# Four moves of order in a fused attention and mixture-of-depths kernel: a query transfer, a scatter, a ranking and a selection

## The chip, the cores and the metric

The kernel runs on one core of a Trainium2 chip. The metric is the device time of one execution in microseconds (us). Each kernel is run several times and the median is given. One further execution is recorded by the hardware profiler; all places in time below count from the first instruction of that record.

The engines are TensorE (PE, with its weight loads as PEld), VectorE (DVE), ScalarE (ACT), GpSimd (POOL) and SyncE (SP). Each works through its own queue in the order in which the program was written, and they wait for one another by semaphores. Transfers are issued from a queue of SP, ACT or POOL and run on 16 DMA engines.

## The reference, cut to what matters

All is float32. Eight batches, eight heads, 1152 keys of 64 values; 576 pooled queries. Then 128 of the 576 rows of each batch are chosen by a score, and go through two layers.

```python
q_pool = q.reshape(B, H, S // 2, 2, D).mean(axis=3)
scores = np.matmul(q_pool, k.transpose(0, 1, 3, 2)) / np.sqrt(D)
attn = np.exp(scores - np.max(scores, axis=-1, keepdims=True))
attn = attn / (np.sum(attn, axis=-1, keepdims=True) + 1e-09)
x = np.matmul(attn, v)                      # (B,H,S,D) -> (B, S, H*D)
scores = np.einsum('bsd,d->bs', x, w_gate)
out = x.copy()
for b in range(B):
    top_idx = np.argpartition(-scores[b], capacity)[:capacity]
    xe = x[b, top_idx]
    ye = np.maximum(xe @ w1, 0.0) @ w2
    g = 1.0 / (1.0 + np.exp(-scores[b, top_idx]))
    out[b, top_idx] = x[b, top_idx] + g[:, None] * ye
```

## The kernel before, in words

The class `_Plain` does the work; `_any_scores` is a second version behind a branch and does not run with these inputs.

**Halves.** The main loop in `run` goes over 32 pairs of heads (four to a batch), each cut into two halves of 288 pooled queries: 64 halves, numbered h. In half h TensorE computes the scores (L877, 72 matmul records), ScalarE takes their exponentials out of PSUM (L884), and TensorE forms the weighted values of half h - 1 (L895, 72 records), which ScalarE copies out (L903, tile `two`) and GpSimd adds up (L905, tile `av`). For the sums of the exponentials, GpSimd adds units of p in three instructions (L916, tile `acc`), DVE folds p and acc (L921) and reduces (L931, tile `sum`); ScalarE lays these side by side (L946, tile `groups`), DVE adds (L952), ScalarE spreads (L961). Further DVE and GpSimd steps transpose (L974), multiply by the gate weights (L984), reduce (L1042) and divide (L1020, tile `x`), and SP stores x to DRAM (L1031). In the first half of each pair the next pair is prepared: GpSimd adds the two rows of each query (L775, `qp`), DVE transposes keys and queries (L778 `kT`, L782 `qT`). There are four PSUM tiles of two banks.

**Order of the work beside it.** What belongs to the choice of rows is written as generators (`routed`, then `layers_of_two`). Three places in each half move them on: "mid" (after the scores), "sums" (after the folds) and "end". `units` takes a generator to its next truthy yield; what it yields says at which place it goes on, and `True` stands for "end". So one more `yield True` moves all that follows by half a pair. In `ending`, after the loop, `pieces(unit, n)` moves a generator by n yields by hand.

**Choosing the rows.** For each batch `routed` sends the 576 scores through DRAM so that they come back shifted per partition (L1089, L1092, tile `line`). The rank of a row is the number of larger scores, counted by ten DVE comparisons, two for each of five tiles t of rows (L1121). For batches 0 to 6 rank and gate go through DRAM (L1150 `row_rank`, L1154 `lines`), and DVE searches in `lines` which row has a given rank (L1185, twice, once with the constant table `token_line`, which holds the number of each row). GpSimd gathers the rows (L1212, `xe`), SP sends them to DRAM and reads them back (L1225 `copy`, L1242), DVE transposes (L1250). For the last batch, 7, DVE builds a matrix of comparisons `pick` in one instruction (L1162), and TensorE multiplies it with `meta`, the number and the gate of each row (L1171, pick stationary, two columns moving); ScalarE copies index and gate (L1178, L1179).

**Layers and scatter.** Batches 0 and 1, and 2 and 3, go through both layers in pairs (`layers_of_two`, seven products in place of eight, L1346). At its end each of the two tokens is scaled and added (`scaled`, L1435), and GpSimd scatters it into out (`written`, L1288); then the sums of weights for the next first layer are loaded again (`load_sums`, L721). Batches 4 to 7 are done in `ending` (L1421 first layer, L1431 second layer), where the products of the second layer come from the generator `second`, and y1, y2, y7 are the places of products 1, 2 and 7.

**Start.** `load_first` loads the first pair without the general path: queries in two parts of three transfers each (L803), keys as three and six columns of both heads (L811), values (L815). `first_queries` (L823, L830, L836, L837) and `first_keys` (L844, L851) add and transpose them.

**Batch 6's place.** With `cuts` of 2 for batch 6, the comparisons of tiles 0 to 2 are written at the end of one half, the others at "mid" of the next, so that all ten stand together in DVE's queue, before the folds of that half.

Of the kernel before, what the change touches and what calls it, by code (L numbers as in the profile page):

```python
# [13 lines left out]
G = 3  # L14
# [525 lines left out]
class _Plain:  # L540
# [85 lines left out]
    def constants(self):  # L626
        nc, const = self.nc, self.const

        token_i = self.small.tile([P, self.NT], I32, name="token_i")
        nc.gpsimd.iota(token_i[:, :], pattern=[[P, self.NT]], base=0, channel_multiplier=1)  # L630
        self.token = const.tile([P, self.NT], F32, name="token")
        nc.vector.tensor_copy(self.token[:, :], token_i[:, :])

        line_i = self.ffn.tile([P, P, 2, self.NT], I32, name="lines", bufs=1)[:, :, 0, :]
        nc.gpsimd.iota(line_i, pattern=[[1, P], [P, self.NT]], base=0, channel_multiplier=0)
        self.token_line = const.tile([P, P, self.NT], F32, name="token_line")
        nc.gpsimd.tensor_copy(self.token_line[:, :, :], line_i)
# [146 lines left out]
    def load_first(self, b, hp):  # L784


        nc, NC, D = self.nc, self.NC, self.D
        room = self.work.tile([P, self.NG, G, 2, self.HALF], F32, name="p")
        room = room.rearrange("p g u j n -> p (g u j n)")
        sixth, n_k = self.QB // 6, 2 * NC * D  # L790
        kn = room[:, 0:n_k].rearrange("p (c j d) -> p c j d", c=NC, j=2)
        n_q = 2 * 4 * sixth * D
        qn = room[0 : 3 * BLK, n_k : n_k + n_q].rearrange("p (a j m d) -> p a j m d", a=2, j=2, d=D)
        qp = room[0 : 3 * BLK, n_k + n_q : n_k + n_q + n_q // 2]
        qp = qp.rearrange("p (a n j d) -> p a n j d", a=2, j=2, d=D)
# [4 lines left out]
        def queries(engine, half):  # L800

            for g in range(3):
                engine.dma_start(  # L803
                    qn[g * BLK : (g + 1) * BLK, half].rearrange("i j m d -> i j (m d)"), of[3 * half + g]
                )

        queries(nc.scalar, 0)
        for a, z in ((0, G), (G, NC)):
            for j, h in enumerate(heads):
                keys = self.k[b, h].rearrange("(p c) d -> p c d", c=NC)  # L810
                nc.sync.dma_start(kn[:, a:z, j, :], keys[:, a:z, :])  # L811
        queries(nc.sync, 1)
        for j, h in enumerate(heads):
            of = self.v[b, h].rearrange("(p c) d -> p c d", c=NC)
            nc.sync.dma_start(v_sb[:, j, :, :], of)  # L815
        return {"k": kn, "q": qn, "qp": qp, "v": v_sb, "b": b, "hp": hp}
# [248 lines left out]
    def routed(self, b, part):  # L1065
# [33 lines left out]
        if b < self.B - 2:  # L1099
            yield True  # L1100
        gate = ffn.tile([P, NT], F32, name="gate")

        small = nc.vector if b == self.B - 1 else nc.gpsimd
        small.tensor_scalar(
            out=gate[:, :], in0=sc, scalar1=-88.0, scalar2=None, op0=ALU.max
        )

        if b == self.B - 1:
            nc.scalar.activation(gate[:, :], gate[:, :], AF.Exp, scale=-1.0)
            yield True  # L1110
        parts = ffn.tile([P, NT, 2], F32, name="rank_parts")
        nc.vector.memset(parts[:, :, :], 0.0)

        nc.vector.memset(parts[self.TAIL :, NF, :], float(Sp))
        rank = ffn.tile([P, NT], F32, name="rank")
        cuts = {self.B - 2: (2,), self.B - 1: (NT,)}.get(b, (1, 3))
        for t, rows in tiles:
            own = t * P + P - 1
            cmp = ffn.tile([P, NT, P], F32, name="pick", bufs=1).rearrange("p t n -> p (t n)")
# [17 lines left out]
        small.tensor_scalar(  # L1137
            out=gate[:, :], in0=gate[:, :], scalar1=1.0, scalar2=None, op0=ALU.add
        )
        if b == self.B - 1:  # L1140
# [15 lines left out]
        for s0, w in self.slots:  # L1156
            index = ffn.tile([P, 1], I32, name="index", bufs=4)
            own_gate = ffn.tile([P, 1], F32, name="own_gate", bufs=4)
            if b == self.B - 1:

                pick = ffn.tile([P, NT, P], F32, name="pick", bufs=1)
                nc.vector.tensor_tensor(  # L1162
                    out=pick[:, :, 0:w],
                    in0=self.token_line[:, s0 : s0 + w, 0].unsqueeze(1).broadcast_to([P, NT, w]),
                    in1=rank[:, :].unsqueeze(2).broadcast_to([P, NT, w]),
                    op=ALU.is_equal,
                )
                yield True
                ps = self.banks()[:, 0, 0:2]
                for t, rows in tiles:  # L1170
                    nc.tensor.matmul(  # L1171
                        ps[0:w, :],
                        lhsT=pick[0:rows, t, 0:w],
                        rhs=meta[0:rows, t, :],
                        start=(t == 0),
                        stop=(t == NT - 1),
                    )
                nc.scalar.copy(index[0:w, :], ps[0:w, 0:1])  # L1178
                nc.scalar.copy(own_gate[0:w, :], ps[0:w, 1:2])  # L1179
            else:  # L1180
# [12 lines left out]
                    )  # L1193

                found = self.small.tile([P, 1], F32, name="found_token")
                search(self.token_line, found)
                nc.vector.tensor_scalar(
                    out=index[0:w, :],
                    in0=found[0:w, :],
# [161 lines left out]
    def layers_of_two(self, tokens):  # L1361
# [148 lines left out]
    def ending(self, halves, old):  # L1510
# [29 lines left out]
        self.gated(halves[-1])  # L1540
        self.scored(halves[-1])
        _, new, _ = self.routing.pop()
        pieces(new, 1)
        pieces(layer, 2)
        for of in (halves[-3]["pair"], last):
# [271 lines left out]
```

## Time and profile before

| | us |
|---|---|
| median of 3 runs | 684.45 |
| lowest, highest | 683.55, 685.75 |
| the profiled execution | 683.79 |
| its span, first to last instruction | 682.0 |
| TensorE busy | 671.3 |
| VectorE busy | 566.1 |
| GpSimd busy | 499.6 |
| ScalarE busy | 454.0 |

The span is what the record covers; 1.8 us of the profiled execution's time lie around it. A line of the timeline gives the start, the time, the engine, the line of the kernel, the operation, the tile written and the tiles read, and how many instructions are merged in it; in brackets the engine's idle time before it and what ended that. A float32 matmul leaves two records. Records of L877 and L895 overlap, since four of them run in different quarters of the array: 72 of them take about 4.37 us though each lasts 0.4.

### The profile page before, as it was taken

How to read it: one execution, taken by the hardware profiler on the slowest of the kernel's cores; microseconds unless marked ns; L12 is line 12 of the kernel's file. 1: busy time of each engine (PE TensorE's matmuls, PEld its weight loads, DVE VectorE, ACT ScalarE, POOL GpSimd, SP SyncE). 2: the span in 40 equal slices, each digit the busy share in tenths (PEclk: the TensorE clock that was granted, in tenths of full speed). 3: DMA queues.
4: the chain of work that ended last, by engine and by line, in shares of the span. 5: the costliest groups of instructions: out<-in, count | busy, mean ns of one | idle time of the engine just before them, and what ended most of it. 6: DMA issues, size and time to landing. Idle time of an engine off the chain costs nothing.

```text
span 682.0 us, 23423 instructions
## 1 busy us (share of the span) xinstructions
PE 671.3 (98%) x9953; PEld 456.7 (67%) x9953; DVE 566.1 (83%) x814; ACT 454.0 (67%) x989; POOL 499.6 (73%) x474
## 2 busy tenths in 40 slices
PE   8999999999999999999999999999999999999996
PEld 6666666665666568676667767767666775657995
DVE  3878998998999887686899987686889998788874
ACT  5677777777877773856777778483777777774220
POOL 4778888889888883866798888384879888867011
PEclk9999999999999999999999999999999999999999
DMA  8888888859896884753888788374588978562311
GB/s 164 168 185 186 221 177 194 160 99 194 197 190 114 175 159 89 202 97 83 225 189 167 146 165 165 81 179 83 122 244 167 161 146 178 129 175 67 64 39 36
DMA packets 391785, 101.99 MB, mean 150 GB/s; under 512 B 371576, under 2 KB 375544, under 8 KB 390648
## 3 DMA queue, kind: packets, MB, share of 16 engines
q1 hardware_dynamic: 390152, 95.93, 66.9%
q0 software_dynamic: 1280, 4.20, 1.8%
q8 instruction: 79, 1.29, 0.8%
q10 hardware_dynamic: 240, 0.30, 0.2%
q14 instruction: 34, 0.28, 0.1%
HBM read 82.77 MB, written 17.62 MB: 147 GB/s over the span
## 4 chain that ended last, share of the span: by engine, by line
PE 79%; DVE 6%; POOL 5%; issue 4%; DMA 3%; ACT 1%; ACTq 0%; POOLq 0%; DVEq 0%
PE ps L877 35%; PE ps L895 35%; PE ps L1346 7%; POOL acc L916 3%; DVE pick L1121 2%; DMA xe<-out_dram,index 1%; PE ps L1421 1%; ACT p L884 1%; DVE kT L778 1%; PE ps L1431 1%; POOL qp L775 1%; DMA p<-in_q_dram 1%; DVE fold L921 1%; POOL out_dram L1288 1%; POOL prod L984 0%
## 5 line engine op out<-in xcount | busy, mean ns | idle before, releaser
L884 ACT ACTIVATE p<-ps 128x576 f32<-128x576 f32 x576 | 320.4, 696 | 4.0 <-PE ps L877 4.0
L916 POOL TENSOR_TENSOR acc<-p 128x576 f32<-128x576 f32 x192 | 275.8, 1465 | 35.1 <-ACT p L884 34.7
L877 PE MATMUL ps<-qT,kT 64*64 64x288 f32 x4608 | 294.0, 404 | 2.1 <-DVE qT L782 1.1
L895 PE MATMUL ps<-p,v_sb 64*64 64x288 f32 x4608 | 291.6, 403 | 0.0
L877 PEld LDWEIGHTS ps<-qT,kT 64*64 64x64 f32 x4608 | 178.1, 132 | 105.7 <-ACT p L884 18.8
L895 PEld LDWEIGHTS ps<-p,v_sb 64*64 64x64 f32 x4608 | 178.2, 133 | 101.3 <-ACT p L884 13.5
L921 DVE TRANSPOSE_TENSOR_REDUCE fold<-p 128x54 f32<-128x1728 f32 x64 | 126.1, 1971 | 39.8 <-ACT p L884 39.8
L921 DVE TRANSPOSE_TENSOR_REDUCE fold<-acc 128x54 f32<-128x1728 f32 x64 | 124.7, 1948 | 17.2 <-POOL acc L916 16.8
L903 ACT COPY two<-ps 128x576 f32<-128x576 f32 x64 | 40.8, 638 | 132.1 <-PE ps L895 127.4
L905 POOL TENSOR_TENSOR av<-two 128x288 f32<-128x288 f32 x64 | 51.2, 800 | 70.7 <-ACT two L903 70.5
L778 DVE STREAM_TRANSPOSE kT<-kb 128x1152 f32<-128x1152 f32 x31 | 73.2, 2360 | 0.0
L984 POOL TENSOR_TENSOR prod<-avb,w_gate 128x288 f32<-128x288 f32 x64 | 51.1, 799 | 0.7 <-DVE red L1042 0.5
L1121 DVE TENSOR_SCALAR_CACHE_REDUCE pick<-line 128x127 f32<-128x127 f32 (+4 forms) x80 | 45.3, 566 | 2.4
L775 POOL TENSOR_TENSOR qp<-qb 128x576 f32<-128x576 f32 x31 | 43.7, 1411 | 2.8 <-DMA qb<-in_q_dram 2.8
L974 DVE STREAM_TRANSPOSE avb<-av 128x288 f32<-128x288 f32 x64 | 28.4, 444 | 18.5 <-POOL av L905 18.5
L961 ACT ACTIVATE sums<-total,tiny 32x18 f32<-32x18 f32 x124 | 38.2, 308 | 5.5 <-DVE total L952 3.6
L1020 POOL TENSOR_TENSOR x<-avb,rec 128x576 f32<-128x576 f32 x30 | 34.8, 1160 | 0.0
L946 ACT COPY groups<-sum 32x36 f32<-32x36 f32 x124 | 27.2, 219 | 5.1 <-DVE sum L931 3.3
L1042 DVE TENSOR_REDUCE red<-prod 128x9 f32<-128x288 f32 x64 | 27.8, 435 | 0.1
L931 DVE TENSOR_REDUCE sum<-fold 128x18 f32<-128x108 f32 x64 | 21.9, 342 | 2.2
L1288 POOL DMA_INDIRECT out_dram<-xe,index x7 | 8.4, 1198 | 20.8 <-DVE xe L1435 10.3
L782 DVE STREAM_TRANSPOSE qT<-qp 128x576 f32<-128x576 f32 x31 | 23.0, 741 | 0.0
(166 smaller groups left out, 437.9 us busy)
## 6 DMA issues: line engine op xcount, KB each, us to landing
kb<-in_k_dram SPq DMA_DIRECT2D x124, 144.0 KB, 3.9
qb<-in_q_dram SPq DMA_DIRECT2D x124, 144.0 KB, 3.6
v_sb<-in_v_dram SPq DMA_DIRECT2D x31, 576.0 KB, 4.8
out_dram<-x SPq DMA_DIRECT2D x128, 72.0 KB, 4.6
tw<-tw SPq DMA_DIRECT2D x8, 1024.0 KB, 6.1
lines<-row_rank SPq DMA_DIRECT2D x7, 640.0 KB, 4.1
w<-in_moe_w_dram SPq DMA_DIRECT2D x8, 512.0 KB, 5.1
tw<-tw SPq DMA_DIRECT2D x8, 512.0 KB, 5.8
```

The lines of the kernel that those rows point to most:

```text
L775: nc.gpsimd.tensor_tensor(out=qp[:, :, :], in0=pair["q"][:, :, 0, :], in1=pair["q"][:, :, 1, :], op=ALU.add)
L778: nc.vector.transpose(kT.rearrange("p (c i g) -> p c g i", c=self.NC, i=BLK), pair["k"].rearrange("p (g c) d -> p c g d", c=self.NC),)
L877: nc.tensor.matmul(sc[keys, j, 0:n], lhsT=pair["kT"][rows, c * P + keys.start : c * P + keys.stop], rhs=pair["qT"][rows, qs], start=True, ...
L884: nc.scalar.activation(p[:, c // G, c % G, :, :], sc[:, :, 0:n], AF.Exp, scale=self.scale)
L895: nc.tensor.matmul(av[j * self.D : (j + 1) * self.D, e, 0:n], lhsT=half["pair"]["v"][keys, j, c, :], rhs=half["p"][keys, c // G, c % G, j, :],
L903: nc.scalar.copy(two[:, :, :], av[:, :, 0:n])
L905: nc.gpsimd.tensor_tensor(out=half["av"][:, :], in0=two[:, 0, :], in1=two[:, 1, :], op=ALU.add)
L916: nc.gpsimd.tensor_tensor(out=acc[:, u, :], in0=units[:, 0, u, :], in1=units[:, 1, u, :], op=ALU.add)
L921: nc.vector.tensor_reduce(fold[:, a, :], of.rearrange("p u (m d) -> p (u m) d", d=BLK), AX.X, ALU.add, apply_transpose=True,)
L984: self.nc.gpsimd.tensor_tensor(out=pair["prod"][:, ns, :], in0=pair["avb"][:, ns, :], in1=self.w_gate[:, hp : hp + 1, :].broadcast_to([P, ...
L1121: nc.vector.tensor_scalar(out=cmp[0:rows, 0 : part.stop - part.start], in0=near[0:rows, part], scalar1=sc[0:rows, t : t + 1], scalar2=None ...
L1346: nc.tensor.matmul(args[0], lhsT=args[1], rhs=args[2], start=k == 0, stop=k == n - 1)
```

## The change

- The third transfer of the first half's queries is issued from SP, between the two small and the two large key transfers, and not from ScalarE's queue.
- `token_line` lies as [tile, place] and not as [place, tile]; the search reads it through a rearranged view.
- The second token of a pair is scattered one half later, by one more `yield True`; the loads behind it go with it.
- Batch 6's comparisons are cut after tile 1, and the rest goes to the end of the next half, not to its "mid". All later steps of batch 6 come a half later, so that the gather is the last step in the loop, and `ending` takes one more piece of it.
- Batch 7: two small gate operations go from DVE to GpSimd, two memsets come earlier; `pick` is made by five comparisons, and stands as the moving operand with `meta` as the stationary one; the result of two rows is copied to SBUF and transposed back. In `ending` product 7 of the second layer comes after these matmuls and before the transpose.

```diff
-        self.token_line = const.tile([P, P, self.NT], F32, name="token_line")
-        nc.gpsimd.tensor_copy(self.token_line[:, :, :], line_i)
+        self.token_line = const.tile([P, self.NT, P], F32, name="token_line")
+        nc.gpsimd.tensor_copy(self.token_line.rearrange("p t i -> p i t"), line_i)
...
-        queries(nc.scalar, 0)
-        for a, z in ((0, G), (G, NC)):
...
-        queries(nc.sync, 1)
+        queries(nc.scalar, 0, (0, 1))
+        keys(0, G)
+        queries(nc.sync, 0, (2,))
+        keys(G, NC)
+        queries(nc.sync, 1, range(3))
...
-        small = nc.vector if b == self.B - 1 else nc.gpsimd
-        small.tensor_scalar(
+        nc.gpsimd.tensor_scalar(
             out=gate[:, :], in0=sc, scalar1=-88.0, scalar2=None, op0=ALU.max
         )
...
-        cuts = {self.B - 2: (2,), self.B - 1: (NT,)}.get(b, (1, 3))
+        cuts = {self.B - 2: (1,), self.B - 1: (NT,)}.get(b, (1, 3))
...
             if t == cuts[-1]:
-                yield "mid"
+                yield mid
...
-                nc.vector.tensor_tensor(
-                    out=pick[:, :, 0:w],
-                    in0=self.token_line[:, s0 : s0 + w, 0].unsqueeze(1).broadcast_to([P, NT, w]),
-                    in1=rank[:, :].unsqueeze(2).broadcast_to([P, NT, w]),
-                    op=ALU.is_equal,
-                )
+                for t, rows in tiles:
+                    nc.vector.tensor_scalar(
+                        out=pick[0:rows, t, 0:w],
+                        in0=self.token_line[0:rows, 0, s0 : s0 + w],
+                        scalar1=rank[0:rows, t : t + 1],
+                        scalar2=None,
+                        op0=ALU.is_equal,
+                    )
                 yield True
-                ps = self.banks()[:, 0, 0:2]
+                ps = self.banks()[:, 0, :]
                 for t, rows in tiles:
                     nc.tensor.matmul(
-                        ps[0:w, :],
-                        lhsT=pick[0:rows, t, 0:w],
-                        rhs=meta[0:rows, t, :],
+                        ps[0:2, 0:w],
+                        lhsT=meta[0:rows, t, :],
+                        rhs=pick[0:rows, t, 0:w],
                         start=(t == 0),
                         stop=(t == NT - 1),
                     )
+                found = ffn.tile([P, NT, P], F32, name="pick", bufs=1)[0:2, 0, 0:w]
+                nc.scalar.copy(found, ps[0:2, 0:w])
+                yield True
+                ps = self.banks()[:, 0, 0:2]
+                nc.tensor.transpose(ps[0:w, :], found, self.ident[0:2, 0:2])
...
             yield True
+            if token is tokens[1]:
+                yield True
             self.written(token, token["index"])
...
         pieces(old, 1)
         pieces(new, 1)
...
-        for to in (y1, y2, y7):
+        for to in (y1, y2):
             copy(to, next(second))
...
         pieces(new, 2)
+        copy(y7, next(second))
+        pieces(new, 1)
         pieces(layer)
```

In the last but one place, the line `pieces(old, 1)` ahead of `pieces(new, 1)` is the one that is added.

More of the change, by code (lines that the diff above doesn't have):

```diff
@@ L798, in load_first, with queries @@
         of = self.q[b, 2 * hp : 2 * hp + 2].rearrange("j (i t m) d -> t i j (m d)", i=BLK, t=6)
-        def queries(engine, half):
-            for g in range(3):
+        def queries(engine, half, groups):
+            for g in groups:
                 engine.dma_start(
@@ L805, in queries, with keys @@
                 )
-        queries(nc.scalar, 0)
-        for a, z in ((0, G), (G, NC)):
+        def keys(a, z):
             for j, h in enumerate(heads):
-                keys = self.k[b, h].rearrange("(p c) d -> p c d", c=NC)
-                nc.sync.dma_start(kn[:, a:z, j, :], keys[:, a:z, :])
-        queries(nc.sync, 1)
+                rows = self.k[b, h].rearrange("(p c) d -> p c d", c=NC)
+                nc.sync.dma_start(kn[:, a:z, j, :], rows[:, a:z, :])
+        queries(nc.scalar, 0, (0, 1))
[3 more added lines that the diff above has]
+        queries(nc.sync, 1, range(3))
         for j, h in enumerate(heads):
@@ L1101, in routed @@
         gate = ffn.tile([P, NT], F32, name="gate")
-        small = nc.vector if b == self.B - 1 else nc.gpsimd
-        small.tensor_scalar(
+        nc.gpsimd.tensor_scalar(
             out=gate[:, :], in0=sc, scalar1=-88.0, scalar2=None, op0=ALU.max
         )
+        parts = ffn.tile([P, NT, 2], F32, name="rank_parts")
+        nc.vector.memset(parts[:, :, :], 0.0)
+        nc.vector.memset(parts[self.TAIL :, NF, :], float(Sp))
         if b == self.B - 1:
@@ L1110, in routed @@
             yield True
-        parts = ffn.tile([P, NT, 2], F32, name="rank_parts")
-        nc.vector.memset(parts[:, :, :], 0.0)
-        nc.vector.memset(parts[self.TAIL :, NF, :], float(Sp))
         rank = ffn.tile([P, NT], F32, name="rank")
-        cuts = {self.B - 2: (2,), self.B - 1: (NT,)}.get(b, (1, 3))
+        cuts = {self.B - 2: (1,), self.B - 1: (NT,)}.get(b, (1, 3))
         for t, rows in tiles:
@@ L1136, in routed @@
                     yield True
-        small.tensor_scalar(
+        nc.gpsimd.tensor_scalar(
             out=gate[:, :], in0=gate[:, :], scalar1=1.0, scalar2=None, op0=ALU.add
@@ L1195, in routed @@
                 found = self.small.tile([P, 1], F32, name="found_token")
-                search(self.token_line, found)
+                search(self.token_line.rearrange("p t i -> p i t"), found)
                 nc.vector.tensor_scalar(
@@ L1542, in ending @@
         _, new, _ = self.routing.pop()
+        pieces(old, 1)
         pieces(new, 1)
```

## The prediction

> **What bounds the kernel now.** I read the page's busy times first, then TensorE's timeline for places where it is not dense, then the timelines of the engines it waited for there.
>
> ```profile
> PE 671.3 (98%) x9953; PEld 456.7 (67%) x9953; DVE 566.1 (83%) x814; ACT 454.0 (67%) x989; POOL 499.6 (73%) x474
> ```
>
> TensorE is busy 671.3 of 682.0 us, at a granted clock of 0.999. An edit on another engine can therefore only win time where TensorE starts late, falls below its pace, or has ended. In the chain of waits an undisturbed stage of scores (L877) or of weighted values (L895), 72 matmul records, takes 4.36 to 4.37 us; a longer stage has a stall in it. The end is fixed: from the last matmuls on, one DVE update, two scatters in a row and a landing, which the change leaves as they are. So I look for stages over 4.37 us which the change touches. The first kind, once at 341 and once at 508 us (timeline of 498 to 516 us, all engines, start and duration in us, idle time and its releaser in brackets):
>
> ```profile
> 501.12 1.71 POOL L1288 DMA_INDIRECT out_dram<-xe,index  x1 [2.41 <-DVE sum L931]
> 502.86 4.15 POOL L916 TENSOR_TENSOR acc<-p 128x576 f32<-128x576 f32 x3
> ...
> 507.04 1.98 DVE L921 TRANSPOSE_TENSOR_REDUCE fold<-acc 128x54 f32<-128x1728 f32 x1 [2.88 <-POOL acc L916]
> ...
> 507.76 4.54 PE L895 MATMUL ps<-p,v_sb 64*64 64x288 f32 x72
> ...
> 509.81 2.32 DVE L778 STREAM_TRANSPOSE kT<-kb 128x1152 f32<-128x1152 f32 x1
> ...
> 511.98 0.75 DVE L782 STREAM_TRANSPOSE qT<-qp 128x576 f32<-128x576 f32 x1
> ```
>
> GpSimd stands still for 2.41 us before the second scatter of a pair, though the xe it writes was ready at 496.2. Its sequencer waits for the semaphore of the gather of the next batch (L1212, landed at 500.31): both touch rows of out. Behind it the additions of L916 are late, so DVE's fold, kT and qT are late, and the scores that could begin at 512.1 begin at 512.87. The stage that starts at 507.76 takes 5.11 us, that at 341.41, of the same make, 5.12.
>
> The second kind, near the end of the main loop (timeline of 576 to 620 us):
>
> ```profile
> 605.55 1.97 DVE L921 TRANSPOSE_TENSOR_REDUCE fold<-p 128x54 f32<-128x1728 f32 x1
> ...
> 609.40 1.63 PE L877 MATMUL ps<-qT,kT 64*64 64x288 f32 x24
> 609.41 0.34 DVE L931 TENSOR_REDUCE sum<-fold 128x18 f32<-128x108 f32 x1
> ...
> 609.78 0.91 ACT L946 COPY groups<-sum 32x36 f32<-32x36 f32 x4 [3.27 <-DVE sum L931]
> ```
>
> The ten comparisons of batch 6 (598.9 to 605.1) stand in DVE's queue ahead of the fold; ScalarE waits 3.27 us for the sum, evacuates late, and the scores from 609.40 to 614.48 take 5.08.
>
> The third and fourth kind, the start and the last batch's picks (timelines of 0 to 16 and 620 to 684 us):
>
> ```profile
> 6.12 0.56 DVE L823 TENSOR_TENSOR p<-p 96x384 f32<-96x384 f32 x1 [6.12 <-DMA p<-in_q_dram]
> ...
> 642.19 1.32 DVE L1162 TENSOR_TENSOR pick<-token_line,rank 128x640 f32<-128x640 f32 x1
> ...
> 643.66 1.33 PE L1171 MATMUL ps<-meta,pick 128*128 128x2 f32 x10 [0.32 <-DVE pick L1162]
> ```
>
> **Second scatter a half later.** GpSimd no longer waits, since the gather has long landed half a pair later. The L916 additions start when their exponentials and the queue allow, about 498.7 in place of 502.86, and end near 502.9. DVE's fold then starts when fold<-p ends (504.16), 2.9 us earlier than 507.04, and kT and qT with it: qT near 509.8, 2 us before TensorE asks for it. Next late would be the scatter itself (1.1 to 1.7 us in the rows), now behind x (L1020) and ahead of the next three additions; these move from 511.1 to about 508.5, still earlier. The reload of the weight sums on SP goes a half later too; its user is over 100 us away. Worth (5.12 - 4.36) + (5.11 - 4.36) = **-1.5**, bounds -1.5 and 0.
>
> **Batch 6's ranking.** Two tiles of comparisons stay (598.9 to 601.35), three (3.7 us) go behind the fold of the next half. GpSimd loses its 2.07 us wait for the gate's exponential, additions end at 601.5, DVE's sum comes near 605.9 in place of 609.4, and ScalarE no longer waits: 5.08 - 4.37 = -0.7. The exponential (0.21) now stands on ScalarE between an evacuation and the nine score exponentials; I take +0.1, bounds 0 and 0.2. Sum **-0.6**.
> What is late next: comparisons 606.5 to 610.2, row_rank out at 610.6 (before, 605.30 out and 611.5 in: 6.2 us), lines in at 616.7. The search waits for it 1 us, ends at 618.6, fold and sum follow to 623.0, avb and red to 623.9. DVE is wanted at 624.35 (av of the last half, 0.7 earlier than 625.07): 0.45 us to spare. The gather goes behind av near 620.2, its copy leaves at 624.1, the read at 626.5 and is in at 629, against L1250 at 632.5; SP is free again before gate_lines (629.3). That is hidden, with 2 to 3 us of cover.
>
> **Start.** The third query transfer leaves SP at about 1.83, as it left ScalarE at 1.78, but now ahead of the two large key transfers, not beside them. By the semaphores in the trace the first four transfers of 96 KB had landed at 4.62, this one at 5.99, the large keys at 6.78 and 8.13. Alone behind the first four it needs 0.5 to 0.7 us (96 KB in 0.92 us for two at once), so 5.2. DVE's addition starts 0.75 earlier, so do the first scores. The transposes of the remaining keys come next (8.78 before): keys still land near 8.13, so they begin near 8.3. **-0.5**, bounds -0.75 and 0.
> [...]
>
> **Batch 7's picks.** Removed from DVE: two gate operations, 0.16 and about 0.19 on its path, since DVE is without a pause from 629.8 to 643.5; picks begin at 641.85. Five comparisons take the place of one of 1.32. The trace has none of this form; nearest are a copy of 128x128 in 0.23 and a counting comparison of 128x127 in 0.35. With 0.07 overlap, five make 0.8 to 1.5; I take 0.9, nearer to the row without accumulation. The seventh product (1.72) moves behind L1171, so TensorE arrives there at 641.54, not 643.27. It waits for the first pick until about 642.2, runs ten records with 128 columns (0.11 each by L1421; 0.126 before) to 643.3, the seventh product to 645.0 and the transposes (0.2) to 645.2; before, 644.92. **+0.3**. Below: picks of 0.1 each and records paced by them, -0.3. Above: matmuls that wait for all five picks at 0.35, +1.5. Index and gather come 0.3 later, 3 us before L1260 asks. The last sum s1 comes at 646.9, TensorE wants it at 647.1: just covered.
> token_line is now read with 512 bytes from element to element in the search. In the trace the search with both inputs strided took 0.78, with one contiguous 0.83, so I take 0; were it to double, batch 6 alone has to pay, 0.8 less its 0.45 to spare. [...]
>
> **Sum.** -1.5 - 0.6 - 0.5 + 0.3 = -2.3 on the profiled execution's 683.79 (span 682.0 and 1.8 around it): 681.5. That execution lies 0.66 below the median of the three runs (684.45; 683.55 to 685.75), from which the same sum gives 682.15. I take 681.8 between them.
>
> **Rivals.**
> 1. The scatter only moves its stall: indirect transfers landed 8 to 9 us after issue at 335 and 501, and it stands in a half that also prepares a pair. For: GpSimd is 73% busy. Against: 4 us of its delay vanish. 683.3.
> 2. The picks cost the upper bound: TensorE idles 2 us where the seventh product filled the gap. For: DVE is without a pause there. 683.0.
> [...]
> 4. The other side: batch 6's lines land late, the search holds DVE's whole queue just before the last batch's chain. Place 616.7, price 1 us for each us over 0.45, and slower than before from 2.8 us late (619.5). Row for it: scatters landed 5 us later than the quick ones; late by 5, 681.8 + 4.5 = 686.3. Against: the same pair of transfers took 6.2 us a half earlier, with more traffic (DMA share 0.75 up to 620 us, 0.34 after).
>
> **Numbers.** Forecast 0.50, rivals 0.15, 0.15, 0.10, 0.10. About 0.3% (2.05 us) is what a measurement can tell: faster means under 682.4. Of the forecast's half 0.4 lies under it, of rival 3 0.05; of rival 4 half is beyond +0.3%. The range leaves out rival 4 and the best bounds: 680.3 to 684.4.
>
> **What would show it.** Scatter: no idle time before L1288 in the main loop, both L895 stages at 4.37. Ranking: sum near 606 on the old clock, no 3 us wait of L946, search idle about 1 us. Start: L823 near 5.4. Picks: TensorE idle 0.5 to 0.8 before L1171, the stretch from the second layer's first product to the next L1421 0.3 longer than 8.72. Wrong, if a stage of over 4.6 us appears behind a moved scatter, if avb of the last half waits for DVE, or if the tail after the last matmul changes.

## The result and the profile after

The changed kernel took 682.54 us (median of 22 runs, 681.9 to 684.8) beside 684.79 us (median of 22 runs, 683.06 to 686.48) for the kernel before on the same chip: a ratio of 0.9971, 95% interval 0.9963 to 0.9979, which is 2.0 us less (1.4 to 2.5); the two medians lie 2.25 us apart. The forecast was 681.8. The profiled execution took 682.70 us (span 680.9), granted clock 0.999. Beside the profiled execution of before (683.79, span 682.0) that is only 1.1 less: the one of before lay 1.0 under its median, the one of after near its own.

Line numbers from `load_first` on are five higher in the changed kernel (L877 is now L882, L895 L900, L916 L921), and those behind the picks eleven to thirteen (L1185 is L1196, L1421 L1434, L1431 L1444). L1162 is now L1167, and L1171 is L1177.

The page's busy times of the changed kernel:

```profile
PE 671.4 (99%) x9954; PEld 445.8 (65%) x9954; DVE 573.9 (84%) x816; ACT 453.9 (67%) x990; POOL 504.0 (74%) x476
```

TensorE has the same work. DVE has 7.8 us more and GpSimd 4.4, and the prediction's sum has no term for either. On DVE it is the search: its fourteen instructions (two for each of seven batches) take 28.3 us together, and took 19.7. With the table in order (e5) they take 24.8, so 3.4 us come from the table's new layout; the other 5.2 are there with the old layout too.

The second scatter, timeline of 497 to 516 us of the changed kernel, all engines (start, duration, engine, line, operation):

```profile
497.89 4.13 POOL L921 TENSOR_TENSOR acc<-p 128x576 f32<-128x576 f32 x3
...
500.36 2.36 DVE L1196 SCALAR_TENSOR_TENSOR pick<-lines,token 128x640 f32<-128x640 f32 x1
...
506.52 4.54 PE L900 MATMUL ps<-p,v_sb 64*64 64x288 f32 x72
507.55 1.06 POOL L1299 DMA_INDIRECT out_dram<-xe,index  x1 [0.15 <-issue]
...
509.79 0.74 DVE L782 STREAM_TRANSPOSE qT<-qp 128x576 f32<-128x576 f32 x1
510.88 4.54 PE L882 MATMUL ps<-qT,kT 64*64 64x288 f32 x72
```

GpSimd's additions begin at 497.89, no longer behind a scatter that waits 2.41 us. The scatter now stands at 507.55 and waits for nothing but its issue. The stage from 506.52 to 510.88 takes 4.36. But qT is ready only 0.35 us before TensorE asks, where the forecast had 2 us: the second half of the search now stands beside the additions, and takes 2.36 us, where it took 0.78 before (L1185 at 501.12).

Batch 6's ranking, the same view from 603 to 621 us:

```profile
603.50 0.34 DVE L936 TENSOR_REDUCE sum<-fold 128x18 f32<-128x108 f32 x1
...
607.36 4.72 PE L882 MATMUL ps<-qT,kT 64*64 64x288 f32 x72
...
611.33 4.14 POOL L921 TENSOR_TENSOR acc<-p 128x576 f32<-128x576 f32 x3
...
614.58 2.07 DVE L1196 SCALAR_TENSOR_TENSOR pick<-lines,token,token_line 128x640 f32<-128x640 f32 x1 [1.32 <-DMA lines<-row_rank]
...
615.43 1.88 POOL L989 TENSOR_TENSOR prod<-avb,w_gate 128x288 f32<-128x288 f32 x1
...
616.76 1.23 DVE L1196 SCALAR_TENSOR_TENSOR pick<-lines,token 128x640 f32<-128x640 f32 x1
...
618.29 1.96 DVE L926 TRANSPOSE_TENSOR_REDUCE fold<-p 128x54 f32<-128x1728 f32 x1
```

The sum is early (603.50) and the scores from 607.36 to 611.90 run through. But the two halves of the search take 2.07 and 1.23 us. The first covers the end of GpSimd's additions (615.47) and the beginning of its prod, which takes 1.88 us here and 0.80 a half earlier (608.70). In the trace of before, the same view has the search at a place where GpSimd stands idle (4.49 us, until 613.87):

```profile
611.54 0.89 DVE L1185 SCALAR_TENSOR_TENSOR pick<-lines,token,token_line 128x640 f32<-128x640 f32 x1 [1.26 <-DMA lines<-row_rank]
...
612.54 0.87 DVE L1185 SCALAR_TENSOR_TENSOR pick<-lines,token 128x640 f32<-128x640 f32 x1
```

The start, timeline of 0 to 16 us of the changed kernel (DVE's first addition; the line of before stood at 6.12):

```profile
5.80 0.55 DVE L828 TENSOR_TENSOR p<-p 96x384 f32<-96x384 f32 x1 [5.80 <-DMA p<-in_q_dram]
```

The last batch's picks, timelines of TensorE and DVE from 630 to 647 us of the changed kernel, in two fences:

```profile
637.10 1.95 PE L1434 MATMUL ps<-p,w 128*128 128x128 f32 x16
640.34 1.34 PE L1177 MATMUL ps<-pick,meta 128*2 128x128 f32 x10 [1.29 <-DVE pick L1167]
641.61 1.99 PE L1444 MATMUL ps<-kT,hT 128*128 128x256 f32 x8
643.54 0.22 PE L1188 MATMUL ps<-ident,pick 2*128 2x2 f32 x1
643.69 2.05 PE L1434 MATMUL ps<-p,w 128*128 128x128 f32 x16
```

```profile
639.91 1.06 DVE L1167 TENSOR_SCALAR pick<-token_line,rank 128x128 f32<-128x128 f32 x5
```

TensorE arrives at the selection 1.29 us before the first pick, and only then does the seventh product (641.61) that used to fill that time.

Where the two traces part, by the start of the same TensorE stage in each:

| stage begins | before | after | difference so far |
|---|---|---|---|
| first scores | 7.65 | 7.49 | -0.16 |
| scores ahead of the first moved scatter | 337.04 | 336.61 | -0.43 |
| scores behind it | 346.53 | 345.34 | -1.19 |
| weighted values at the second moved scatter | 507.76 | 506.52 | -1.24 |
| scores behind it | 512.87 | 510.88 | -1.99 |
| scores beside batch 6's ranking | 609.40 | 607.36 | -2.04 |
| weighted values behind them | 614.48 | 611.90 | -2.58 |
| second layer's first product | 636.20 | 633.65 | -2.55 |
| next L1421 / L1434, behind the selection | 644.92 | 643.69 | -1.23 |
| end of the span | 682.0 | 680.9 | -1.1 |

2.6 us are won up to the ending, and 1.3 of them are lost within it.

### The profile page after: what moved, and what is told of

It is laid out like the page before. It is cut to its first block, busy times and chain, and to the rows that moved or that the text cites. A ratio compares the mean times of both kernels' runs of the same rounds, so it can differ in the third digit from the quotient of the medians.

```text
span 680.9 us, 23432 instructions
## 1 busy us (share of the span) xinstructions
PE 671.4 (99%) x9954; PEld 445.8 (65%) x9954; DVE 573.9 (84%) x816; ACT 453.9 (67%) x990; POOL 504.0 (74%) x476
## 3 DMA queue, kind: packets, MB, share of 16 engines
q8 instruction: 79, 1.29, 0.7%
## 4 chain that ended last, share of the span: by engine, by line
PE 85%; DVE 7%; issue 3%; DMA 2%; POOL 1%; ACT 1%; SPq 0%; DVEq 0%; POOLq 0%; ACTq 0%
PE ps L882 38%; PE ps L900 37%; PE ps L1357 7%; DVE fold L926 2%; DVE pick L1125 2%; PE ps L1444 1%; ACT p L889 1%; DMA lines<-row_rank 1%; POOL acc L921 1%; DMA p<-in_q_dram 1%; DVE acc L1453 0%; DMA out_dram<-xe,index 0%; DMA out_dram<-lines,index 0%; DVE kT L778 0%; PE ps L1434 0%
## 5 line engine op out<-in xcount | busy, mean ns | idle before, releaser
L921 POOL TENSOR_TENSOR acc<-p 128x576 f32<-128x576 f32 x192 | 278.7, 1479 | 29.2 <-ACT p L889 28.9
L882 PE MATMUL ps<-qT,kT 64*64 64x288 f32 x4608 | 293.0, 404 | 0.7 <-DVE token L632 0.5
L900 PE MATMUL ps<-p,v_sb 64*64 64x288 f32 x4608 | 291.3, 403 | 0.0
L882 PEld LDWEIGHTS ps<-qT,kT 64*64 64x64 f32 x4608 | 172.8, 132 | 108.5 <-ACT p L889 18.8
L900 PEld LDWEIGHTS ps<-p,v_sb 64*64 64x64 f32 x4608 | 172.6, 133 | 107.0 <-ACT p L889 14.0
L1196 DVE SCALAR_TENSOR_TENSOR pick<-lines,token,token_line 128x640 f32<-128x640 f32 x7 | 18.1, 2587 | 3.4 <-DMA lines<-row_rank 3.3
```

The source lines that it names most:

```text
L882: nc.tensor.matmul(sc[keys, j, 0:n], lhsT=pair["kT"][rows, c * P + keys.start : c * P + keys.stop], rhs=pair["qT"][rows, qs], start=True, ...
L900: nc.tensor.matmul(av[j * self.D : (j + 1) * self.D, e, 0:n], lhsT=half["pair"]["v"][keys, j, c, :], rhs=half["p"][keys, c // G, c % G, j, :],
L921: nc.gpsimd.tensor_tensor(out=acc[:, u, :], in0=units[:, 0, u, :], in1=units[:, 1, u, :], op=ALU.add)
```

## The experiments

Three theories stood against each other; the expectations give their numbers. Theory 1: the parts add, each with the size in the two traces. Theory 2: executions of one kernel differ by half a microsecond and more at the same stalls, so that a pair of traces does not settle the sizes. Theory 3: the old selection is at times followed by a stretch at half clock, which the change avoids. A ratio is that of a kernel to the kernel before on the same chip. The parts alone ran on one chip (before: 683.46, 35 runs), the variants of the change on a second (before: 683.95, 15 runs), the last ones on a third (before: 683.29, 23 runs).

**e1: the scatter alone.**

```diff
+            if token is tokens[1]:
+                yield True
             self.written(token, token["index"])
```

> The kernel before with the second scatter a half later, and nothing else. Theory 1 (the stall is GpSimd's wait for a gather's landing, and goes whole): the two long stages of L895 at 341 and 508 us fall from 5.12 and 5.11 to 4.37, time -1.5 us, ratio 0.9978. Theory 2 (the wait follows the transfers' traffic, so that most executions lose more by it than the profiled one did): the same two stages, but the median falls by 2 to 2.5 us, ratio 0.9965, and the spread of the times shrinks.

Measured: 682.29 us, 0.9981 (0.9970 to 0.9992). Timeline of TensorE:

```profile
506.21 4.54 PE L895 MATMUL ps<-p,v_sb 64*64 64x288 f32 x72
510.57 4.54 PE L877 MATMUL ps<-qT,kT 64*64 64x288 f32 x72
```

From one start to the next 4.36, and 4.37 at the other pair; the scores near 608 keep their 5.12. By the ratio this part is worth 1.3 us by itself (0.5 to 2.1), by the medians 1.2: the prediction's -1.5 holds, and theory 2's ratio of 0.9965 lies outside the interval. Here too the second half of the search takes 2.37 us in place of 0.78, with the table in order.

**e2: the start alone** (the whole edit of `load_first`, nothing else).

```diff
+        queries(nc.scalar, 0, (0, 1))
+        keys(0, G)
+        queries(nc.sync, 0, (2,))
+        keys(G, NC)
+        queries(nc.sync, 1, range(3))
```

> The kernel before with the third query transfer on SP, and nothing else. Theory 1 (the transfer is ahead of the large keys and lands 0.3 us earlier, as in the changed kernel): DVE's first addition L823 starts near 5.8 in place of 6.12, the scores 0.2 to 0.5 us earlier, time -0.3 us. [...]

Measured: 683.71 us, 1.0003 (0.9990 to 1.0017). The addition starts at 5.59 and the first scores at 7.33. That looks like a gain beside 6.12 and 7.65, but isn't one: the traces with the old start have the addition at 5.62, 5.73, 5.75, 6.12 and 6.13, those with the new one between 5.23 and 6.08, and the first scores lie at 7.26 to 7.66 and 6.92 to 7.61. The start differs by 0.4 us and more between executions of the same order of transfers. On the mean of five and of nine traces the addition starts at 5.87 and 5.65, the first scores at 7.43 and 7.34: of the forecast's 0.5 us about 0.1 is seen. The interval of the time (0.7 us less to 1.2 us more) would not exclude 0.5.

**e3: batch 6's ranking alone.**

```diff
-        cuts = {self.B - 2: (2,), self.B - 1: (NT,)}.get(b, (1, 3))
+        cuts = {self.B - 2: (1,), self.B - 1: (NT,)}.get(b, (1, 3))
...
-                yield "mid"
+                yield mid
...
+        pieces(old, 1)
         pieces(new, 1)
```

> The kernel before with the ranking of batch 6 cut after tile 1 and its rest a half later, and nothing else; the search reads contiguously, as before. Theory 1 (the 0.5 us that DVE is late at the end in the changed kernel come from the strided search): scores near 609 take 4.5 in place of 5.08, the search takes 0.8 to 0.9 after POOL's additions, the gap ahead of L1171 stays within 0.3 of 0.32, time -0.5 us. Rival (the later search makes DVE late whatever it reads): the scores' gain comes back at L1171, gap 0.7 to 0.9, time -0.1 us or no change.

Measured: 683.95 us, 1.0003 (0.9990 to 1.0015). The scores near 608 take 4.37, so the stall goes as predicted. Yet the search takes 1.72 and 1.23 us though it reads the table as before: it is the place, beside GpSimd's additions, that makes it long (0.89 and 0.87 in before, where GpSimd stands idle). And in this execution something else follows (timeline of TensorE, then the windows view of TensorE alone with stretch, length, busy time and matmuls, granted clock, DMA share and GB/s):

```profile
641.96 1.33 PE L1171 MATMUL ps<-meta,pick 128*128 128x2 f32 x10 [0.72 <-ACT p L1458]
643.22 3.39 PE L1421 MATMUL ps<-p,w 128*128 128x128 f32 x16
```

```profile
634.00:643.60 9.60, 8.88 (x56) 1.00 0.18 31
643.70:647.00 3.30, 3.30 (x17) 0.50 0.28 79
```

The changed kernel in the same stretch, same view:

```profile
643.70:647.00 3.30, 3.30 (x24) 1.00 0.22 58
```

After a gap of 0.72 us and the ten records of the old selection the clock is 0.50 (the view of 640 to 650 us has a mean of 0.83, which makes 3.4 us at half clock); sixteen matmuls take 3.18 from start to start instead of 1.89, and the loss is about 1.6 us. So this one trace can't be used for the price of the part. Five of its twelve executions have a mean clock of 0.996 or less, and of the kernel before on the same chip 5 of the 34 under 700 us. The other seven have a median of 683.28, and the other 29 of before 683.23: without those too the part alone shows no gain, as the rival forecast. The gap of 0.72 is in the rival's range too, but the kernel before has gaps from 0.25 (e1 and e2, with the ending as before) to 0.66 (e12), so one trace doesn't show that the ranking made it. e10 takes this up.

**e4: batch 7's picks alone** (selection, table layout and the seventh product's place).

```diff
...
-                        ps[0:w, :],
-                        lhsT=pick[0:rows, t, 0:w],
-                        rhs=meta[0:rows, t, :],
+                        ps[0:2, 0:w],
+                        lhsT=meta[0:rows, t, :],
+                        rhs=pick[0:rows, t, 0:w],
...
-        for to in (y1, y2, y7):
+        for to in (y1, y2):
             copy(to, next(second))
...
         pieces(new, 2)
+        copy(y7, next(second))
+        pieces(new, 1)
```

> The kernel before with the whole of batch 7's selection (gate on GpSimd, five comparisons, table stationary, other layout of the table, seventh product later), and nothing else. Theory 1 (the loss is the seventh product that no longer fills TensorE's wait, and part of it was DVE's lateness from the ranking): the gap ahead of the selection's matmuls is 0.8 us, time +0.8 us. Rival (all of it belongs to the selection): gap 1.3 us, time +1.3 us. My forecast of 0.5 to 0.8 us for the gap and +0.3 would need +0.3.

Measured: 684.95 us, 1.0029 (1.0008 to 1.0049): by itself this part costs 2.0 us by the ratio (0.5 to 3.3), 1.5 by the medians. Timeline of TensorE:

```profile
642.76 1.34 PE L1172 MATMUL ps<-pick,meta 128*2 128x128 f32 x10 [1.24 <-DVE pick L1162]
```

The gap of 1.24 us is there without the other parts, and the ending is 1.27 longer than before (22.82 beside 21.55). The rest comes from the main loop: the two stages at L895 grow from 5.12 and 5.11 to 5.66 and 5.63. With the table's layout the first half of the search takes 4.92 us at 490 (4.45 before), so GpSimd waits 1.65 us for the gather's index (1.16 before), and the scatter behind the gather comes later. Here the record names what the scatter waits for, the landing of the gather, as the prediction has it (timeline of GpSimd):

```profile
501.56 1.28 POOL L1294 DMA_INDIRECT out_dram<-xe,index  x1 [2.84 <-DMA xe<-out_dram,index]
```

Added up, the four parts alone (e1 to e4) would make the kernel 0.16% slower, and together they make it 0.29% faster. The four intervals together allow about 0.3%, so the parts do not add, against theory 1: the stride costs 1.06 us at the two L895 stages only where the scatter is not moved.

**e9: the changed kernel once more**, on the second chip, as the base of the next three.

> The changed kernel itself, beside the three others on their chip. All theories: ratio 0.997 within 0.001. Theory 3: at most one execution in ten has a mean clock of 0.995 or less, since 128 columns move in the selection. Theory 1 says nothing of the clock and expects as many as in the kernel before.

Measured: 682.41 us, 0.9979 (0.9969 to 0.9989): 1.5 us less than before, with a gap of 1.28 ahead of the selection. None of its ten executions has a mean clock of 0.995 or less.

**e6: the seventh product back ahead of the selection.**

```diff
-        for to in (y1, y2):
+        for to in (y1, y2, y7):
             copy(to, next(second))
...
-        pieces(new, 2)
-        copy(y7, next(second))
-        pieces(new, 1)
+        pieces(new, 3)
```

> The changed kernel with the seventh product back ahead of the selection, the copy and the transpose following its matmuls at once. Theory 1 (the seventh product's place makes the loss): no wait before L1177, a wait of 0.4 to 0.5 us for the copy before the transpose, the next L1434 0.9 to 1.1 us earlier after the first product than the 10.04 of the changed kernel, time -1.0 us against it. Rival (DVE is late by what is behind the picks, so TensorE waits elsewhere): no change.

Measured: 681.32 us, 0.9956 (0.9942 to 0.9970), 1.1 less than e9. Timeline of TensorE:

```profile
639.00 1.95 PE L1434 MATMUL ps<-p,w 128*128 128x128 f32 x16
640.88 1.34 PE L1177 MATMUL ps<-pick,meta 128*2 128x128 f32 x10
642.57 0.22 PE L1188 MATMUL ps<-ident,pick 2*128 2x2 f32 x1 [0.34 <-ACT pick L1185]
642.71 2.05 PE L1434 MATMUL ps<-p,w 128*128 128x128 f32 x16
```

No wait ahead of the selection; only 0.34 for the copy (here L1185) between selection and transpose (L1188). The stretch from the second layer's first product (633.82) to the next L1434 is 8.89, beside 10.04 in the changed kernel and 8.72 before.

**e7: the old selection and table in the changed kernel** (seventh product ahead of it, gate on DVE).

```diff
...
-                        ps[0:2, 0:w],
-                        lhsT=meta[0:rows, t, :],
-                        rhs=pick[0:rows, t, 0:w],
+                        ps[0:w, :],
+                        lhsT=pick[0:rows, t, 0:w],
+                        rhs=meta[0:rows, t, :],
...
```

> The changed kernel with the selection of batch 7 as before (pick stationary with two columns moving, one comparison, gate on DVE, contiguous table, seventh product ahead of it): scatter, ranking and start alone. Theory 1 (the selection as changed only costs): the scores near 609 and the L895 stages are short as in the changed kernel, the gap ahead of L1171 is 0.7 as with the ranking alone, time 1.0 us under the changed kernel, and no more executions with a low clock than before. [...]

Measured: 681.81 us, 0.9963 (0.9949 to 0.9977), 0.6 less than e9, with a gap of 0.49. None of its six executions has a mean clock of 0.996 or less, so theory 3 gets no support from it. At the medians the kernel is thus faster without the changed selection and table than with them.

**e8: the best of both**: five comparisons and the gate on GpSimd stay; the pick is the stationary operand again, with no copy and transpose; the seventh product goes first; the table is as before.

```diff
...
+                ps = self.banks()[:, 0, 0:2]
...
+                        ps[0:w, :],
+                        lhsT=pick[0:rows, t, 0:w],
+                        rhs=meta[0:rows, t, :],
...
+        for to in (y1, y2, y7):
...
```

> The changed kernel with pick stationary again (two columns moving, no copy and no transpose), the seventh product ahead of it, the search contiguous as before; gate on GpSimd and five comparisons kept. Theory 1: the selection ends within 0.1 us of the kernel before, 8.7 us after the first product, time -1.3 us against the changed kernel. [...]

Measured: 681.07 us, 0.9952 (0.9938 to 0.9966), 1.3 less than e9 and the lowest ratio of all. Timeline of TensorE:

```profile
642.33 1.26 PE L1177 MATMUL ps<-meta,pick 128*128 128x2 f32 x10
643.52 2.05 PE L1429 MATMUL ps<-p,w 128*128 128x128 f32 x16
```

No wait at all, and the stretch is 8.16 (from 635.36), 0.56 less than before the change. The profiled execution itself had a mean clock of 0.995, and its first sixteen records of L882 (at 7.61) take 1.72 us, where those of L877 take 1.20 in before, so its absolute times are late throughout.

**e5: the changed kernel with the table's old layout.**

```diff
-        self.token_line = const.tile([P, self.NT, P], F32, name="token_line")
+        self.token_line = const.tile([P, P, self.NT], F32, name="token_line")
...
-                search(self.token_line.rearrange("p t i -> p i t"), found)
+                search(self.token_line, found)
```

> The changed kernel with token_line laid out as before: the search reads contiguously, the five comparisons read it with 20 bytes from element to element. Theory 1 (512 bytes from element to element make the search 0.5 us longer, and that is all of what DVE's lateness at the end has from the layout): searches of batches 0, 1, 3 take 0.83 in place of 1.3, that of batch 6 1.5 in place of 2.0, the picks come 0.3 to 0.5 earlier on TensorE's clock, the gap ahead of L1177 falls from 1.28 to 0.8 to 1.0, time -0.3 to -0.5 us against the changed kernel, ratio to before 0.9970 to 0.9975. Rival (the comparisons with 20 bytes between elements lose it again): no change.

Measured: 682.44 us, 0.9980 (0.9968 to 0.9992), in time not to be told from the change. In the trace the undisturbed searches are back at 0.83 us, batch 6's takes 1.44 and 1.23, the five comparisons take 1.29 instead of 1.06, and the gap falls from 1.29 to 0.87 (timeline of TensorE):

```profile
640.16 1.34 PE L1177 MATMUL ps<-pick,meta 128*2 128x128 f32 x10 [0.87 <-DVE pick L1167]
```

So the layout accounts for 0.4 us of the gap, and the stretch from the second layer's first product to the next L1434 falls with it, from 10.04 to 9.62. The median doesn't show that gain.

**e10: the combined kernel with batch 6's ranking as before, and e11: the combined kernel again**, on the third chip.

```diff
-        cuts = {self.B - 2: (1,), self.B - 1: (NT,)}.get(b, (1, 3))
+        cuts = {self.B - 2: (2,), self.B - 1: (NT,)}.get(b, (1, 3))
...
-                yield mid
+                yield "mid"
...
-        pieces(old, 1)
```

> The combined kernel (pick stationary, seventh product ahead, contiguous search, gate on GpSimd, five comparisons, scatter and start as changed) with the ranking of batch 6 as before. Theory 1 (the ranking wins 0.5 us at the scores near 609 and gives 0.1 to 0.2 back at the picks): the scores take 5.08 again, the picks' gap is as long or shorter, time +0.3 to +0.4 us against the combined kernel on the same chip. Rival (the ranking gives back all that it wins, as it seemed when alone): no change, ratio to before as that of the combined kernel.

> The combined kernel a second time, on the chip of the two before. Ratio to before 0.9952 within 0.0012; selection without a wait of over 0.3 us ahead of L1177; ends within 8.3 us of the first product of the second layer.

Measured: e10 681.39 us, 0.9973 (0.9962 to 0.9983); e11 680.94 us, 0.9962 (0.9948 to 0.9975). The ratio of e11 is within its expectation. The ranking is worth 0.45 at the medians, but the intervals overlap. In the traces it is 0.57: from those scores to L1429 behind the selection 35.00 and 34.43 us, and the picks begin as early as without it (5.76 and 5.82 us after the second layer's first product). Timeline of TensorE of e10, with the stall that the ranking removes:

```profile
609.02 3.39 PE L882 MATMUL ps<-qT,kT 64*64 64x288 f32 x48 [0.28 <-ACT two L908]
```

**e12: the kernel before, one more look**, unchanged.

> The kernel before once more, for one look at a second execution: which of its stages differ between executions. Theory 1: the two L895 stages at 341 and 508 us take 5.0 to 5.2 and the scores near 609 5.1, as in the first profile; the start of the scores differs by up to 0.4 us between executions, with the place at which the clock is granted. Theory 2 (the wait for the gather varies): the two L895 stages differ by 0.5 us or more from 5.12.

Measured: 685.86 us, span 684.0. Timeline of GpSimd, then the windows view of TensorE alone:

```profile
501.67 1.05 POOL L1288 DMA_INDIRECT out_dram<-xe,index  x1 [3.41 <-DVE pick L1185]
```

```profile
645.90:649.30 3.40, 3.40 (x16) 0.50 0.30 82
```

The scatter waited 3.41 us here (2.41 in the first profile), and the two L895 stages take 4.99 and 5.44 (5.12 and 5.11). In this trace the stalls differ by 0.1 and 0.3, less than theory 2 asked for. The trace of e3 has the same code up to batch 6, and there the first stage takes 4.96 and the second (timeline of TensorE)

```profile
507.17 4.55 PE L895 MATMUL ps<-p,v_sb 64*64 64x288 f32 x72
511.54 1.86 PE L877 MATMUL ps<-qT,kT 64*64 64x288 f32 x25
```

4.37 from start to start: no stall at all, though GpSimd waited 2.27 us before that scatter. So theory 2 is right in that the stall at 508 goes from nothing to 1.1 us between executions. In the four traces with scatter and table as before (the first, e2, e3, e12) the two stalls together are 1.50, 1.33, 0.60 and 1.70 us, 1.3 on the mean, which is what e1 measured.

In e12 the gap ahead of L1171 is 0.66 (0.32 in the first), and a stretch at half clock follows (0.50 from 645.90 to 649.30) and costs about 1.65, as in e3. That accounts for most of the distance between this execution and the first profile.

## Why the prediction was right or wrong

**Second scatter: right, with less to spare than forecast.** -1.50 in the pair of traces, about -1.3 alone (e1) and on the mean of the traces. None of the things named as next late came. But qT was to be ready 2 us before TensorE asks, and is ready 0.35 us before (0.75 with the table in order, e1 and e5): the forecast left out that the second half of the search, now beside the additions, takes 2.36 us in place of 0.78.

**Batch 6's ranking: the gain right, one step wrong.** The stall went (-0.54 in the traces, where -0.6 was forecast; -0.45 to -0.57 by e10 and e11). But the step "0.45 us to spare" failed: the last avb begins 0.74 us after the av that it reads (0.26 in before), so it waits for DVE, which the prediction had named as a sign of being wrong (timeline of DVE of the changed kernel; the av ends at 622.50):

```profile
623.24 0.47 DVE L979 STREAM_TRANSPOSE avb<-av 128x288 f32<-128x288 f32 x1
```

The prediction took the search's two halves at about 0.9 each from the rows of before, though the change moves them to a place where GpSimd adds. They take 2.07 and 1.23; at the same place with the table in order 1.32 to 1.52 and 1.22 to 1.23 (e5, e8, e11). What makes DVE late, however, is the stride and not the place, as the beginning of that avb shows, in us from the ending's first product:

| | ranking as before | ranking moved |
|---|---|---|
| table in order | 1.96 (before), 1.83 (e1), 1.82 (e2), 1.98 (e10), 2.29 (e12) | 1.94 (e5), 1.93 (e7), 1.92 (e8), 1.89 (e11), 2.17 (e3) |
| table strided | 2.40 (e4) | 2.45 (the change), 2.44 (e6), 2.39 (e9) |

e12 and e3, both with the scatter not moved, lie between, and why is open. The transfers took what was forecast (the search is idle for 1.32 us, forecast about 1), so rival 4 did not come. Beside each other both engines are slower here: the first half of the search takes 1.72 us beside the additions with the table in order (e3), and 0.89 where GpSimd stands idle (before), and GpSimd's prod beside the search goes from 0.80 to 1.88 us (the change). What makes them so is not shown.

**Start: wrong as far as the runs show.** The step that failed is "alone behind the first four it needs 0.5 to 0.7 us": the addition was to start near 5.4, 0.75 earlier, and starts at 5.65 on the mean of nine traces, 0.2 earlier than in the five with the old order; the first scores gain 0.1. Alone it gave 1.0003 (e2), and the variation of the start by 0.4 us hides whatever is left. That the query lands no earlier (rival 3, 0.10) is nearer to what was measured than the forecast; no run shows a reason for it.

**Batch 7's picks: the mechanism right, the size wrong.** The wait in TensorE was forecast at 0.5 to 0.8 us, the cost at +0.3; measured were a gap of 1.29 and +1.32, near the price of rival 2. The comparisons took about what was forecast (1.06 for five, 0.9 forecast). What failed first is "picks begin at 641.85": they begin at 639.91, which is 642.46 counted from the old start of the second layer's first product (2.55 later). With the table in order they begin at 642.00 on the same count (e5), so most of that delay is the stride again. The terms behind it were too small as well: the ten records take 1.27 us to the next start (1.1 forecast), and the seventh product 1.93 (1.7). Of the 1.3 us, 0.4 lie in the table's layout by way of the late DVE (e5); putting the seventh product back in the gap returns 1.1 (e6). These two overlap, and don't add to more than the gap. With both put right and the pick stationary again, the ending is 0.56 shorter than before (e8, e11).

**The table's stride: wrong.** Taken as 0, from two rows of before that don't have this form; a search that GpSimd doesn't disturb takes 1.31 to 1.36 us instead of 0.83, +0.5 each. Up to the ending that is hidden when the scatter is moved, and not when it isn't (e4).

**Sum.** -1.5 - 0.5 + 1.3 - 0.2 (start) - 0.3 (shorter stages that the change doesn't touch, which differ between executions) is -1.2, and the pair of traces shows -1.1. The forecast of -2.3 had 0.3 to 0.5 too much at the start and missed 1.0 in the ending. So it is luck, as far as the runs show, that the medians of the first chip lie 2.25 apart and so close to it: the terms as measured make half of that, and on the second chip the same change gave -1.5. The forecast of 681.8 is 0.7 below the measured 682.54 because it started from 683.79 and 684.45, while the median of before came out at 684.79.

**What stays open.** The first chip's medians differ by 2.25 where traces and second chip say 1.1 to 1.5. The two chips don't contradict each other: their intervals, 1.4 to 2.5 and 0.8 to 2.1 us, overlap. Half-clock stretches in before may be part of the difference. Of the 114 executions under 700 us with the old selection and a gap ahead of it whose clock is on record, 17 have a mean clock of 0.996 or less; of 62 with the table as the stationary operand, 2. Five of the 17 are among the twelve of e3, which has the longest gap. But e7 shows none in six, and 17 in 114 at 1.6 us each are a mean of 0.24 us, not enough for the difference. It is not settled.

## What to carry to other kernels

A product that fills a wait is moved only when the input that is waited for has really come earlier: here that alone cost 1.1 us, where all the other edits together gained 2.6 up to the ending. When an instruction of DVE like this search is moved, look at what GpSimd does at its new place, for the durations of the old place need not go with it: its second half took 0.78 us in before and 2.36 beside the additions. The same holds for GpSimd's work that comes to stand beside it: prod took 0.80 and 1.88. Gains of a third of a per cent are judged by medians of many executions, and by one part at a time, taken out of the whole as well as put in alone; two profiles of one kernel, on two chips, differed by 2 us here, and a stall of 1.1 us in one trace was missing from another.

## What the runs showed of the hardware

In the clock records of the two traces of before and of the change the granted clock is 1.0 for 675.84 us (before, until 680.98) and 672.43 us (the change, until 679.33), and 0.5 from there to the end; the two lengths differ by 3.41. The switch comes 5.29 and 4.88 us after the end of the last matmul (675.69 and 674.45). Earlier stretches at half clock stand in the windows views of e3 (0.50 from 643.70 to 647.00) and e12 (0.50 from 645.90 to 649.30). What sets the place of a switch is not shown.

In e3 a gap of 0.72 us and in e12 one of 0.66 us with 1.3 us of matmuls of two columns came ahead of the half clock, at a price of about 1.6 us. A gap of 0.49 us with the same matmuls was not followed by such a stretch in e7, whose profiled execution has a mean clock of 0.999, nor one of 0.32 us in before (1.0 until 680.98). A gap of 1.29 us ahead of matmuls of 128 columns was not followed by half clock either (the change, 1.00 from 643.70 to 647.00). Whether the length of the gap, its place or the shape of the matmuls decides is not shown: no run was made to test it.

A table of 640 elements read with 512 bytes from element to element costs DVE's search 0.5 us more than in order (1.31 beside 0.83, the change and e5), and five comparisons of 128 elements read with 20 bytes from element to element cost 1.29 together (e5), beside 1.06 in order (the change).
